# Deadlines for ScalarE's and VectorE's order, and seven products in two of three blocks of one set

## The chip, the core and the metric

The kernel runs on one NeuronCore of one Trainium2 chip. The metric is device time in microseconds (us) of one execution, as the median of several runs; lower is better. Five engines work side by side, each through its own instructions in order: TensorE (PE; its weight loads are listed as PEld), VectorE (DVE), ScalarE (ACT), GpSimd (POOL) and SyncE (SP, which issues most DMAs). They wait for each other by semaphores.

## The reference

Causal attention with a learned decay, then two feed-forward layers, all in fp32:

```python
scores = q @ k.T / sqrt(D) + (cum_i - cum_j)        # cum: running sum of log f, causal mask
x = softmax(scores) @ v                             # 4 x 8 heads, 576 x 64, to 2304 x 512
h = x @ w_in0;  x = (h - tanh(h)) @ w_out0          # 512 -> 2048 -> 512
h = x @ w_in1;  out = (h * sigmoid(h)) @ w_out1     # 512 -> 2048 -> 512
```

## The kernel before

Every large product is made of three products of fp32r parts: each operand is split into a rounded high part (a copy or cast on ScalarE) and the rest (a subtraction on VectorE), and TensorE multiplies high by high, high by low and low by high.

Attention fills about the first 260 us. The two layers follow, in 24 units: unit u is a layer (12 units each), a set of 512 of the 2048 hidden columns (four sets in a layer) and one of three blocks of 768 tokens. Units 0 to 11 are the first layer, 12 to 23 the second; units 12, 13 and 14 are the second layer's first set. Units 0 to 2 run interleaved with the attention's end; `joint()` makes the rest.

A unit's first product (512 model columns to hidden columns, `h_step`, L646) runs as seven block products in place of eight, by Strassen's scheme in Winograd's form: seven steps of 12 matmuls 384 columns wide, on sums of blocks. Its second product (`c_step`, L708) is made in seven steps too where the unit is not in `PLAIN`: 12 matmuls of 384 columns a step in the first layer, 18 of 256 in the second (L729). A unit in `PLAIN` makes it in eight steps without block sums (`plain_c`, L750, matmuls at L769): four steps of 12 matmuls and four of 6, all 512 columns wide, in the second layer. Before, `PLAIN` is units 12 to 14.

In TensorE's order the seven steps of unit u's first product alternate with the seven (or eight) steps of unit u-1's second product, one each in turn. The stretch between the first h_step of unit u and that of unit u+1 is called unit u's stretch below; it holds the second product of unit u-1.

Around this, ScalarE and VectorE do, for each unit:

- bending: the running sums that Winograd's form wants (`seed` and `cp`, copies within PSUM on ScalarE; L1016, L937), Tanh or Silu, and the sums `two` (L940) of bent quarters: two in a plain unit, six in one of seven products;
- splitting the second product's operands into high and low, `gr` (L980 ScalarE, L981 VectorE): four of 768 columns in a plain unit, seven in one of seven products, through a ring of three tiles;
- gathering the second product into `x` (L1016 to L1065), in the first layer's last set with four more sums `mix` (L1047), two of which read a PSUM bank that the next unit's second product will write;
- in units 12 to 14 alone, `make` (L882): two sums (L890) and seven operands `xr` (L905 ScalarE, L902 VectorE), which are spilled to DRAM. Later units load them with a DMA.

Beside this the weights are decoded, once for each chunk q (two chunks to a set) and each matrix m: float64 bits come in by DMA, `scale` (L203) on ScalarE, `shift`, `exponent`, `low`, `join` (L207 to L226) on VectorE, four sums of 256 columns (L230), and the split into high (L247) and low (L249). A plain set's second matrix keeps the undone blocks, without the sums (L239, L241). All decodes share the scratch tiles `wa`, `wb` and `ws`, so they follow one another in the order written.

All of these are written as tasks: the time at which each is wanted (`when`, in steps of 2.08 us), engine, cost, what it reads and writes. `planned` (L1116) puts them in order before the launch. It goes through a model of the engines: TensorE, SyncE and the DMA tasks run in the order of `when`; on VectorE and ScalarE the task that is ready with the least due time is next, where due is `when` plus a hand-set `spare`. Tasks marked `keen` (those that read or write TensorE's banks) may hold an engine idle until they are ready. The order found is what the program issues; at run time each engine keeps it.

```python
now = [n for r, n in known if r <= t]
n = min(now, key=lambda n: tasks[n][7])            # least due
if not tasks[n][6] and tasks[n][7] > t - 2:        # not keen: leave room for a keen one
```

Of the kernel before, what the change touches and what calls it, by code (L numbers as in the profile page):

```python
# [8 lines left out]
F32R = mybir.dt.float32r  # L9
# [29 lines left out]
S0 = U0 // 3  # L39
PLAIN = (12, 13, 14)  # L40
PLAINSETS = {u // NB for u in PLAIN if u >= NB * NSET}
EARLIER = 5
MIXED = {u // NB for u in PLAIN if u < NB * NSET}

# [4 lines left out]
def forgetting_attention_two_ffn(  # L49
# [106 lines left out]
    def wload(q, m, parts=(0, 1)):  # L156
# [20 lines left out]
    )  # L177
# [418 lines left out]
    def ftile(u, what):  # L596
        k = u % 2
        if what == "12":
            if "12" not in small_tiles:
                small_tiles["12"] = pools["xb"].tile([P, 2, 2, TH], F32, tag="xo7", name="f_12")  # L600
            return small_tiles["12"][:, k]
        if what == "21":
            return flat(f"21_{k}", "hp", f"h{k}")
        if what == "1":
            return flat("1", "tp", "t0")
        if what == "22":
            return flat("22", "tp", "t1")
        if what == "tmp":
            if what not in small_tiles:
                g = gfree.pop(0)  # L610
                small_tiles[what] = pools[f"gp{g // 2}"].tile([P, 2, TH], F32, tag=f"gh{g}", name="f_tmp")
                small_tiles["spare"] = g
            return small_tiles[what]
        return flat(what, "xt", {"a": "xt1", "b": "xt2"}[what])
# [49 lines left out]
    def aside_tile():  # L664

        if "tile" not in aside:
            g = small_tiles["spare"]
            aside["tile"] = pools[f"gp{g // 2}"].tile([P, 2, TH], F32, tag=f"gl{g}", name="aside")
        return aside["tile"]
# [40 lines left out]
    def c_step(u, k):  # L710
        l, i = units[u][0], csteps(u)[k]
        t = gtile(gop(u, k))
        if u in PLAIN:
            return plain_c(u, *i, t)
        acc, fresh = cbank(u, i)
        at = WAT[l][i]
        ws = [[w[:, 0] for w in place(2 * (u // NB) + j, at)] for j in range(2)]
        for d in range(3 if l else 2):
            ds = slice(d * P, d * P + P)
            for j, (wh, wl) in enumerate(ws):  # L720
                gh, gl = (t[:, e, j] for e in range(2))
# [12 lines left out]
    def place(q, at):  # L734

        if at >= 11:
            if q % NSLOT < 2:
                return [w[:, 7:8] for w in wtile(q, 0)]
            if "spare" not in wtiles:
                g = small_tiles["spare"]  # L740
                t = pools[f"gp{g // 2}"].tile([P, 2, 256], F32R, tag=f"gl{g}", name="wspare")
                wtiles["spare"] = [t[:, 0:1], t[:, 1:2]]
            return wtiles["spare"]
        return [w[:, at - 8:] for w in extra(q, 1)] if at >= 8 else [w[:, at:] for w in wtile(q, 1)]
# [5 lines left out]
    def plain_c(u, c, a, t):  # L750
# [4 lines left out]
        for d in range(2 - a if l else 2):  # L755
            for j in range(2):
                q = 2 * (u // NB) + j
                gh, gl = (t[:, e, j] for e in range(2))
                if l:
                    ds = slice((2 * a + d) * P, (2 * a + d) * P + P)  # L760
# [35 lines left out]
    def joint():  # L796
# [5 lines left out]

        def task(when, eng, cost, fn, reads=(), writes=(), keen=False, spare=0):

            tasks.append((when, eng, cost, fn, reads, writes, keen, when + spare))

# [16 lines left out]
        def decode(q, m):  # L823
# [17 lines left out]
            groups = [0, 1, 2] if m and q // 2 in MIXED else [0, 1]  # L841
            behind = m and q % 2 and 3 * (q // 2) - 1 in PLAIN
            for g in [1, 3, 4, 5] if behind else groups:
# [4 lines left out]
        def spread(t0, t1, jobs, since):  # L848
# [3 lines left out]
            for e, c, fn, r, w, tag in jobs:  # L852
                if e == "D":
                    task(t - 6, e, c, fn, r, w)
                    continue
                t = max(t, since.get((w[0][:3], tag), t))
                task(t, e, c, fn, r, w, False, 3)
                if e == "V":
                    t += (t1 - t0) * c / total
# [22 lines left out]
        def make(u):  # L882
# [6 lines left out]
            def total(when, to, p, r, op=MINUS):  # L889
                task(t0 + when, "V", W2, lambda: tt_(q[to](), q[p](), q[r](), op), (key[p], key[r]), (key[to],), False, 2)  # L890

# [4 lines left out]
            for k, i in enumerate(STEPS):  # L896
# [7 lines left out]

                task(when, "A", N2, lambda n=n, f=f: copy(ring_tile(n)[:, 0], q[f]()), (key[f],), (kr,), False, 2)  # L905
                task(when + 0.1, "V", W2, low, (key[f], kr), (kr,), False, 2)


        for u in range(U0, len(units) + 1):
            t0 = base[u]  # L910
            if u < len(units):
# [27 lines left out]
                def two(when, to, p, r, op, kt, kp, kr, keen=True):  # L939
                    task(when, "V", W2, lambda: tt_(to, p, r, op), (kp, kr), (kt,), keen, 0 if keen else 2.5)  # L940

# [34 lines left out]
                for k, i in enumerate(order):  # L976
                    n = opno(u) + k
                    g, (frm, kf), kg = gtile(n), src[i], n % 3
                    w = t0 + when[k] + (more if k else 0)
                    task(w, "A", N2, lambda g=g, f=frm: copy(g[:, 0], f), (kf,), (("gh", kg),), False, 2)  # L980
                    task(w + 0.1, "V", W2, lambda g=g, f=frm: tt_(g[:, 1], f, rd(g[:, 0]), MINUS),  # L981
                         (kf, ("gh", kg)), (("gl", kg),), False, 2)
            v = u - 1
# [19 lines left out]
            for k, i in enumerate(csteps(v)):  # L1003
                if plain_:
                    n, kd = gop(v, k), (ky, kz)[i[1]]
                    r = [kd, ("gh", n % 3), ("gl", n % 3)] + [w for j in range(2) for g in (range(1) if l else range(3)) for w in wkeys(q + j, 1, g)]
                    task(t0 + min(2 * k + 1, 14), "P", 1, lambda v=v, k=k: c_step(v, k), r, (kd,))
                    continue
# [3 lines left out]
                when = t0 + k if last else t0 + 2 * k + 1  # L1012
                task(when, "P", 1, lambda v=v, k=k: c_step(v, k), r, (kd,))

# [15 lines left out]
            if l == 0:  # L1030
# [14 lines left out]
                else:  # L1045
                    def mix(when, spare, to, frm, r, op, keys, kt):
                        task(when, "V", W2, lambda: tt_(to() if callable(to) else to, frm, r, op), keys, (kt,), False, spare)  # L1047

                    mix(t0 + 11.5, 4, aside_tile, xs[22], xs[21], MINUS, (kx[22], kx[21]), "aside")
                    mix(t0 + 12.5, 3, xs[22], xs[22], xs[12], PLUS, (kx[22], kx[12]), kx[22])  # L1050
                    mix(t0 + 14.05, 1.2, xs[12], xs[12], ys, MINUS, (kx[12], ky), kx[12])
                    mix(t0 + 14.06, 1.2, xs[21], xs[21], ys, PLUS, (kx[21], ky), kx[21])
                task(t0 + (14.5 if s < NSET - 1 else 13), "S", 0, lambda b=b: aside_store(b), ("aside",), (("t1", b),))
# [62 lines left out]
    def planned(tasks):  # L1116
# [12 lines left out]
        writer, readers, deps = {}, {}, []  # L1129
        for n, (when, eng, cost, fn, reads, writes, keen, due) in enumerate(tasks):  # L1130
            d = {writer[k] for k in reads if k in writer}
# [11 lines left out]
        queue = {e: [n for n, t in enumerate(tasks) if t[1] == e] for e in free}  # L1143

        def ready(n):
            if all(d in end for d in deps[n]):
                return max([end[d] + lag(n, d) for d in deps[n]] + [tasks[n][0] - EARLY])

        while any(queue.values()):
            best = None  # L1150
            for e, waiting in queue.items():
# [4 lines left out]
                now = [n for r, n in known if r <= t]  # L1156
                n = min(now, key=lambda n: tasks[n][7])
                if not tasks[n][6] and tasks[n][7] > t - 2:
                    soon = [r for r, k in known if tasks[k][6] and t < r < t + tasks[n][2] - 0.2]
                    if soon:  # L1160
                        t = min(soon)
                        n = min((k for r, k in known if r <= t and tasks[k][6]), key=lambda n: tasks[n][7])
                if best is None or t < best[0]:
                    best = t, e, n
            t, e, n = best
            queue[e].remove(n)
            end[n] = t + tasks[n][2]
# [441 lines left out]
```

## Time and profile before

| | |
|---|---|
| median of 3 runs | 914.43 us (914.15 to 914.65) |
| the profiled execution | 914.77 us, of which 913.0 us lie between its first and last instruction (the span) |
| TensorE busy, by matmuls | 897.7 us, 98% of the span |
| VectorE busy | 771.3 us, 84% |
| ScalarE busy | 594.6 us, 65% |
| mean granted TensorE clock | 0.996 of full speed |

A matmul's listed duration includes a modelled end that overlaps the next one's start, so the price of a step of several matmuls is read from start to start. VectorE's and ScalarE's listed durations overlap their successors a little too.

### The profile page before, as it was taken

The numbers are of one execution on the slowest core, as the hardware profiler recorded it, in microseconds if no ns is written. First come the engines' busy times: TensorE is split into PE (matmuls) and PEld (weight loads), VectorE is DVE, ScalarE is ACT, GpSimd is POOL, SyncE is SP. The second block draws the span as 40 slices with busy tenths as digits, with TensorE's granted clock in tenths as the row PEclk, the third lists the DMA queues.
The fourth block names the chain that finished last, engine by engine and source line by source line (L and its number), as shares of the span: only waits on it lengthen the run. The fifth ranks groups of instructions, "written<-read, shape, count | busy, mean of one in ns | idle before, by whom it ended". The sixth has DMA issues, their size and how long they took to land.

```text
span 913.0 us, 15853 instructions
## 1 busy us (share of the span) xinstructions
PE 897.7 (98%) x5898; PEld 842.2 (92%) x5898; DVE 771.3 (84%) x1297; ACT 594.6 (65%) x992; POOL 161.3 (18%) x242
## 2 busy tenths in 40 slices
PE   9999999999999999999999989999999999999997
PEld 6777777799999999999999979898899999999997
DVE  7799999789888999998999989875598889876647
ACT  5888888766565767666776767665565566555443
POOL 8999999400000000000000000000000000000000
PEclk9999999999999999999999989999999999999999
DMA  5424533567457777787768656676567666555753
GB/s 164 154 98 155 167 121 103 193 245 314 196 217 265 237 252 259 236 302 280 251 241 287 220 207 252 238 267 235 190 230 282 205 225 225 180 201 176 233 167 117
DMA packets 51101, 196.01 MB, mean 215 GB/s; under 512 B 9744, under 2 KB 15120, under 8 KB 50992
## 3 DMA queue, kind: packets, MB, share of 16 engines
q1 hardware_dynamic: 50744, 194.72, 60.2%
q8 instruction: 46, 0.75, 0.3%
q10 hardware_dynamic: 280, 0.28, 0.1%
q14 instruction: 31, 0.25, 0.1%
HBM read 151.98 MB, written 41.88 MB: 212 GB/s over the span
## 4 chain that ended last, share of the span: by engine, by line
PE 93%; DVE 4%; ACT 2%; issue 1%; POOL 0%; DVEq 0%; ACTq 0%; POOLq 0%
PE h L656 32%; PE a L729 28%; PE a L769 5%; PE s L1294 5%; PE t L1341 5%; PE a L431 5%; PE out_t L1397 5%; PE h L475 3%; PE s L1286 2%; PE h L461 1%; PE out_t L1425 1%; DVE x L1047 1%; DVE gr L981 0%; DVE x L1024 0%; PE out L1397 0%
## 5 line engine op out<-in xcount | busy, mean ns | idle before, releaser
L656 PE MATMUL h<-xr,wh 128*128 128x384 f32 x1176 | 299.8, 335 | 1.0 <-ACT h L937 0.9
L656 PEld LDWEIGHTS h<-xr,wh 128*128 128x128 f32 x1176 | 210.6, 189 | 3.4 <-ACT h L937 1.6
L656 PE MATMUL h<-xr,wl 128*128 128x384 f32 x588 | 197.0, 335 | 0.0
L656 PEld LDWEIGHTS h<-xr,wl 128*128 128x128 f32 x588 | 110.6, 188 | 0.0
L981 DVE TENSOR_TENSOR gr<-f,gr 128x768 fp32r<-128x768 f32 x102 | 97.0, 953 | 14.5 <-ACT gr L980 14.5
L980 ACT CAST gr<-f 128x768 fp32r<-128x768 f32 x102 | 85.5, 838 | 33.3 <-PE a L729 29.5
L1024 DVE TENSOR_TENSOR x<-a,x 128x768 f32<-128x768 f32 (+1 forms) x64 | 59.4, 930 | 28.2 <-PE a L729 27.7
L1315 ACT ACTIVATE p<-p,mn 128x128 f32<-128x128 f32 (+3 forms) x128 | 71.2, 558 | 17.1 <-DVE mn L1307 14.4
L729 PE MATMUL a<-wh,gr 128*128 128x256 f32 x420 | 80.8, 282 | 0.0
L729 PE MATMUL a<-gr,wh 128*128 128x384 f32 x288 | 75.2, 341 | 4.7 <-ACT a L1016 4.1
L1329 POOL TENSOR_SCALAR p<-p,sm 128x128 f32<-128x128 f32 (+3 forms) x128 | 72.7, 584 | 7.7 <-DVE sm L1326 7.2
L1307 DVE CUSTOM_DVE_ANT_0 p<-s,mask 128x128 f32<-128x128 f32 (+3 forms) x128 | 59.6, 479 | 14.3 <-PE s L1294 14.2
L729 PEld LDWEIGHTS a<-wh,gr 128*128 128x128 f32 x420 | 67.5, 190 | 0.0
L1016 ACT COPY a<-a 128x768 f32<-128x768 f32 x43 | 33.7, 784 | 41.8 <-PE a L729 38.5
L729 PE MATMUL a<-weh,gr 128*128 128x256 f32 x312 | 60.2, 282 | 0.3 <-DVE x L1024 0.3
L729 PE MATMUL a<-wl,gr 128*128 128x256 f32 x210 | 59.4, 283 | 0.6 <-DVE wl L249 0.6
L937 ACT COPY h<-h 128x768 f32<-128x768 f32 x42 | 32.9, 784 | 39.6 <-PE h L656 39.2
L729 PEld LDWEIGHTS a<-gr,wh 128*128 128x128 f32 x288 | 53.0, 191 | 5.9 <-ACT a L1016 4.8
L729 PE MATMUL a<-gr,weh 128*128 128x384 f32 x216 | 54.8, 334 | 0.0
L1236 POOL TENSOR_TENSOR kqs<-kqraw,kqs 128x288 fp32r<-128x288 f32 (+1 forms) x62 | 53.8, 889 | 1.3
L937 ACT COPY f<-h 128x768 f32<-128x768 f32 x42 | 33.7, 802 | 30.4 <-PE h L656 22.7
L729 PEld LDWEIGHTS a<-weh,gr 128*128 128x128 f32 x312 | 50.2, 190 | 0.6 <-issue 0.5
(167 smaller groups left out, 2106.3 us busy)
## 6 DMA issues: line engine op xcount, KB each, us to landing
xr<-xd SPq DMA_DIRECT2D x126, 768.0 KB
raw<-w_in SPq DMA_DIRECT2D x32, 512.0 KB
raw<-w_out SPq DMA_DIRECT2D x32, 512.0 KB
xd<-xo SPq DMA_DIRECT2D x21, 768.0 KB
xd<-xr SPq DMA_DIRECT2D x21, 768.0 KB
kqraw<-kq SPq DMA_DIRECT2D x16, 608.0 KB
aside<-aside SPq DMA_DIRECT2D x15, 384.0 KB
vraw<-v SPq DMA_DIRECT2D x16, 320.0 KB
```

The costliest lines, as they stand in the source:

```text
L431: nc.tensor.matmul(dst, w, m, start=first and r == 0, stop=last and r == 2)
L656: nc.tensor.matmul(dst[:, j, 0:TH], w[:, ds], m[:, d], start=i in (1, 5) and d == r == 0, stop=d == 1 and r == 2, skip_group_check=True,)
L729: nc.tensor.matmul(dst, w, m, start=fresh and (l == 0 or d != 1) and j == r == 0, stop=j == 1 and r == 2, skip_group_check=True,)
L769: nc.tensor.matmul(dst, w, m, start=fresh and j == r == 0, stop=last and j == 1 and r == 2, skip_group_check=True)
L937: task(when, "A", N2, lambda: copy(to, frm), (kf,), (kt,), True)
L980: task(w, "A", N2, lambda g=g, f=frm: copy(g[:, 0], f), (kf,), (("gh", kg),), False, 2)
L981: task(w + 0.1, "V", W2, lambda g=g, f=frm: tt_(g[:, 1], f, rd(g[:, 0]), MINUS), (kf, ("gh", kg)), (("gl", kg),), False, 2)
L1024: task(when, "V", n, lambda: tt_(to, *((frm, to) if op == PLUS else (to, frm)), op), (kf, kx[c]), (kx[c],), True)
L1236: eng.tensor_tensor(lo[:, c0:c1], raw[p][:, c0:c1], rd(hi[:, c0:c1]), ALU.subtract)
L1307: nc.vector.tensor_tensor_reduce(out=pt.rearrange("p (g c) -> p g c", g=2) if i == 4 else pt, in0=src, in1=m, op0=ALU.add, op1=ALU.min, sc ...
L1315: nc.scalar.activation(pt, pt, AF.Exp, bias=mn, scale=-1.0, accum_out=sums[:, n // 3 % 5, n % 3, 0:1],)
L1329: nc.gpsimd.tensor_scalar(pt, pt, sm[:, j:j + 1], 1.0, ALU.mult, ALU.mult)
```

## The change

`PLAIN` becomes unit 13 alone. Units 12 and 14 make their second product in seven steps, as later units of the second layer do. Unit 13 still makes all eight block products, but since the set's second matrix is now stored as block sums, with the one undone block that the sums lack kept in a spare column block of the first matrix's tile (`place`), its matmuls are 256 columns wide: 24 in a long step, 12 in a short one. Unit 12's first c_step gains two matmuls of 256 columns that write one whole PSUM bank, and with that waits for what still reads that bank; the previous unit's two last `mix` sums do.

In `planned` the hand-set `spare` is gone. Each ScalarE, VectorE and DMA task gets a latest end: TensorE's tasks have their `when`, and from each task back to what it depends on the cost and the lag are subtracted. The ready task with the least latest end is next; an engine holds for a task that becomes ready soon where that task would miss its latest end behind the chosen one, and the chosen one can wait. This goes for all tasks, of all units from 3 to 23.

```diff
-PLAIN = (12, 13, 14)
-PLAINSETS = {u // NB for u in PLAIN if u >= NB * NSET}
+PLAIN = (13,)
+PLAINSETS = {s for s in range(NSET, 2 * NSET) if all(NB * s + b in PLAIN for b in range(NB))}
-MIXED = {u // NB for u in PLAIN if u < NB * NSET}
+MIXED = {u // NB for u in PLAIN} - PLAINSETS
...
-        (((0, 4, 1),), ((8, 3, 5),), (), ((1, 1, 2),), ((2, 2, 3),), ((0, 1, 1),)),
+        (((0, 4, 1),), ((8, 3, 5),), ((11, 1, 0),), ((1, 1, 2),), ((2, 2, 3),), ((0, 1, 1),)),
...
         acc, fresh = cbank(u, i)
+        if k == 0 and l and units[u - 1][0] == 0:
+
+            w = place(2 * (u // NB), WAT[l][i])[0][:, 0]
+            for c in range(2):
+                nc.tensor.matmul(csums(u)[1][:, 0, 256 * c:256 * c + 256], t[:, 0, 0, 0:P], w, start=c == 0, stop=True,
+                                 skip_group_check=True)
...
         if at >= 11:
-            if q % NSLOT < 2:
-                return [w[:, 7:8] for w in wtile(q, 0)]
...
+            return [w[:, 7:8] for w in wtile(min(q % NSLOT, 1), 0)]
...
+                if l and u // NB in MIXED:
+                    ds = slice((2 * a + d) * P, (2 * a + d) * P + P)
+                    for k, at in enumerate(((11, 1), (0, 2))[i]):
+                        wh, wl = (w[:, 0] for w in place(q, at))
+                        for r, (w, m) in enumerate(((gh[:, ds], wh), (gh[:, ds], wl), (gl[:, ds], wh))):
+                            nc.tensor.matmul(
+                                acc[:, d, 256 * k:256 * k + 256], w, m, start=fresh and j == k == r == 0,
+                                stop=last and j == 1 and r == 2, skip_group_check=True,
+                            )
+                    continue
...
-            tasks.append((when, eng, cost, fn, reads, writes, keen, when + spare))
+            tasks.append((when, eng, cost, fn, reads, writes, keen))
...
-            behind = m and q % 2 and 3 * (q // 2) - 1 in PLAIN
+            behind = m and l and q % 2 and 3 * (q // 2) - 1 in PLAIN and q // 2 not in MIXED
...
-                task(when, "P", 1, lambda v=v, k=k: c_step(v, k), r, (kd,))
+                kd = (kd, kz) if k == 0 and v == NB * NSET and v - 1 not in PLAIN else (kd,)
+                task(when, "P", 1, lambda v=v, k=k: c_step(v, k), r, kd)
...
+        latest = [t[0] if t[1] == "P" else 1e9 for t in tasks]
+        for n in reversed(range(len(tasks))):
+            for d in deps[n]:
+                if tasks[d][1] != "P":
+                    latest[d] = min(latest[d], latest[n] - lag(n, d) - tasks[d][2])
...
-                n = min(now, key=lambda n: tasks[n][7])
-                if not tasks[n][6] and tasks[n][7] > t - 2:
-                    soon = [r for r, k in known if tasks[k][6] and t < r < t + tasks[n][2] - 0.2]
-                    if soon:
-                        t = min(soon)
-                        n = min((k for r, k in known if r <= t and tasks[k][6]), key=lambda n: tasks[n][7])
+                n = min(now, key=lambda n: latest[n])
+
+                soon = [(r, k) for r, k in known if t < r < t + tasks[n][2] - 0.1 and latest[k] + behind < t + tasks[n][2]
+                        and latest[n] + behind > r + tasks[k][2]]
+                if soon:
+                    t, n = min(soon)
```

## Rows read from the trace of the kernel before

**Rows 1.** The page: the span, and each engine's busy us, share and instructions.

```profile
span 913.0 us, 15853 instructions
PE 897.7 (98%) x5898; PEld 842.2 (92%) x5898; DVE 771.3 (84%) x1297; ACT 594.6 (65%) x992; POOL 161.3 (18%) x242
```

**Rows 2.** Windows of units 10 to 13, 15 to 17: start:end, length, busy by engine.

```profile
core 0: us, PE busy (x) PEld busy (x) DVE busy (x) ACT busy (x) POOL busy (x), PEclk, DMA share, GB/s
...
464.62:493.74 29.12, 29.12 (x169) 29.12 (x169) 26.59 (x32) 19.65 (x26) 0.00 (x0) 1.00 0.79 279
493.74:523.60 29.86, 29.40 (x170) 29.08 (x170) 28.19 (x35) 20.33 (x27) 0.00 (x0) 1.00 0.67 234
523.60:560.27 36.67, 32.44 (x169) 31.71 (x169) 33.03 (x39) 24.93 (x31) 0.00 (x0) 0.91 0.51 201
560.27:591.50 31.23, 31.23 (x158) 28.16 (x158) 27.59 (x37) 20.67 (x27) 0.00 (x0) 1.00 0.71 274
...
622.74:653.99 31.25, 31.25 (x158) 28.18 (x156) 15.61 (x20) 15.48 (x19) 0.00 (x0) 1.00 0.61 212
653.99:684.53 30.54, 29.95 (x211) 29.65 (x210) 27.73 (x40) 21.14 (x29) 0.00 (x0) 1.00 0.57 196
684.53:714.17 29.64, 29.64 (x213) 29.64 (x211) 25.11 (x30) 16.45 (x22) 0.00 (x0) 1.00 0.73 261
```

**Rows 3.** Windows, their sum: units 4 to 11, then units 12 to 14.

```profile
sum 233.88, PE 233.42 PEld 232.90 DVE 221.98 ACT 161.15 POOL 0.00; mean PE 29.18 PEld 29.11 DVE 27.75 ACT 20.14 POOL 0.00
...
sum 99.14, PE 94.91 PEld 88.06 DVE 83.65 ACT 66.33 POOL 0.00; mean PE 31.64 PEld 29.36 DVE 27.88 ACT 22.11 POOL 0.00
```

**Rows 4.** Timeline of PE at unit 12's stall: start, us, what, [idle before <-releaser].

```profile
533.66 0.69 PE L729 MATMUL a<-gr,wh 128*128 128x384 f32 x1 [3.66 <-ACT a L1016]
534.92 0.69 PE L729 MATMUL a<-gr,wh 128*128 128x384 f32 x1 [0.58 <-DVE gr L981]
```

**Rows 5.** Windows behind that stall; the granted clock stands third from the end.

```profile
536.00:538.00 2.00, 2.00 (x8) 2.00 (x8) 1.47 (x2) 0.00 (x0) 0.00 (x0) 0.50 0.29 120
```

**Rows 6.** Timeline of ACT there: the copy that TensorE waits for.

```profile
532.80 0.80 ACT L1016 COPY a<-a 128x768 f32<-128x768 f32 x1
```

**Rows 7.** Timeline of DVE there.

```profile
514.19 1.22 DVE L214 SCALAR_TENSOR_TENSOR wb<-raw,wb 128x1024 f32<-128x1024 uint32 x1
...
527.77 0.95 DVE L1047 TENSOR_TENSOR x<-x,a 128x768 f32<-128x768 f32 x1
528.64 0.95 DVE L1047 TENSOR_TENSOR x<-x 128x768 f32<-128x768 f32 x1
529.51 0.95 DVE L902 TENSOR_TENSOR xr<-f_tmp,xr 128x768 fp32r<-128x768 f32 x1
...
530.38 0.95 DVE L1047 TENSOR_TENSOR x<-x,a 128x768 f32<-128x768 f32 x1
...
533.91 0.95 DVE L981 TENSOR_TENSOR gr<-f,gr 128x768 fp32r<-128x768 f32 x1
```

**Rows 8.** Timeline of PE at unit 12's plain steps, then at seven-product steps of unit 16.

```profile
562.36 0.39 PE L769 MATMUL a<-wh,gr 128*128 128x512 f32 x1
...
565.12 0.51 PE L656 MATMUL h<-xr,wh 128*128 128x384 f32 x2
...
567.22 0.39 PE L769 MATMUL a<-wh,gr 128*128 128x512 f32 x1
...
568.61 0.51 PE L656 MATMUL h<-xr,wh 128*128 128x384 f32 x2
...
703.55 0.28 PE L729 MATMUL a<-weh,gr 128*128 128x256 f32 x1
...
705.70 0.52 PE L656 MATMUL h<-xr,wh 128*128 128x384 f32 x2
```

**Rows 9.** Timeline of DVE in unit 14's stretch: weight decoding.

```profile
604.63 1.09 DVE L230 TENSOR_TENSOR ws<-ws 128x256 f32<-128x256 f32 x3
605.64 0.69 DVE L207 TENSOR_SCALAR wa<-raw 128x1024 uint32<-128x1024 uint32 x1
...
607.30 1.23 DVE L214 SCALAR_TENSOR_TENSOR wb<-raw,wb 128x1024 f32<-128x1024 uint32 x1
...
621.23 1.23 DVE L226 TENSOR_TENSOR ws<-wa,wb 128x1024 f32<-128x1024 f32 x1
```

More of the change, by code (lines that the diff above doesn't have):

```diff
@@ L611, in ftile @@
                 small_tiles[what] = pools[f"gp{g // 2}"].tile([P, 2, TH], F32, tag=f"gh{g}", name="f_tmp")
-                small_tiles["spare"] = g
+                small_tiles["aside"] = g
             return small_tiles[what]
@@ L666, in aside_tile @@
         if "tile" not in aside:
-            g = small_tiles["spare"]
+            g = small_tiles["aside"]
             aside["tile"] = pools[f"gp{g // 2}"].tile([P, 2, TH], F32, tag=f"gl{g}", name="aside")
@@ L736, in place @@
         if at >= 11:
-            if q % NSLOT < 2:
-                return [w[:, 7:8] for w in wtile(q, 0)]
[L739 to L743, printed above, removed]
+            return [w[:, 7:8] for w in wtile(min(q % NSLOT, 1), 0)]
         return [w[:, at - 8:] for w in extra(q, 1)] if at >= 8 else [w[:, at:] for w in wtile(q, 1)]
@@ L801, in joint, with task @@
         tt_, copy = nc.vector.tensor_tensor, nc.scalar.copy
-        def task(when, eng, cost, fn, reads=(), writes=(), keen=False, spare=0):
-            tasks.append((when, eng, cost, fn, reads, writes, keen, when + spare))
+        def task(when, eng, cost, fn, reads=(), writes=(), keen=False):
+            tasks.append((when, eng, cost, fn, reads, writes, keen))
         def dve(n):
@@ L856, in spread @@
                 t = max(t, since.get((w[0][:3], tag), t))
-                task(t, e, c, fn, r, w, False, 3)
+                task(t, e, c, fn, r, w)
                 if e == "V":
@@ L889, in total @@
             def total(when, to, p, r, op=MINUS):
-                task(t0 + when, "V", W2, lambda: tt_(q[to](), q[p](), q[r](), op), (key[p], key[r]), (key[to],), False, 2)
+                task(t0 + when, "V", W2, lambda: tt_(q[to](), q[p](), q[r](), op), (key[p], key[r]), (key[to],))
             task(t0 - 4, "D", 3, lambda: aside_load(b, q["11"]()), (("t1", b),), (key["11"],))
@@ L903, in low @@
                     spill(n)
-                task(when, "A", N2, lambda n=n, f=f: copy(ring_tile(n)[:, 0], q[f]()), (key[f],), (kr,), False, 2)
-                task(when + 0.1, "V", W2, low, (key[f], kr), (kr,), False, 2)
+                task(when, "A", N2, lambda n=n, f=f: copy(ring_tile(n)[:, 0], q[f]()), (key[f],), (kr,))
+                task(when + 0.1, "V", W2, low, (key[f], kr), (kr,))
         for u in range(U0, len(units) + 1):
@@ L939, in two @@
                 def two(when, to, p, r, op, kt, kp, kr, keen=True):
-                    task(when, "V", W2, lambda: tt_(to, p, r, op), (kp, kr), (kt,), keen, 0 if keen else 2.5)
+                    task(when, "V", W2, lambda: tt_(to, p, r, op), (kp, kr), (kt,), keen)
                 cp(t0 + 1.05, zs, ys, kz, ky)
@@ L979, in joint @@
                     w = t0 + when[k] + (more if k else 0)
-                    task(w, "A", N2, lambda g=g, f=frm: copy(g[:, 0], f), (kf,), (("gh", kg),), False, 2)
+                    task(w, "A", N2, lambda g=g, f=frm: copy(g[:, 0], f), (kf,), (("gh", kg),))
                     task(w + 0.1, "V", W2, lambda g=g, f=frm: tt_(g[:, 1], f, rd(g[:, 0]), MINUS),
-                         (kf, ("gh", kg)), (("gl", kg),), False, 2)
+                         (kf, ("gh", kg)), (("gl", kg),))
             v = u - 1
@@ L1005, in joint @@
                     n, kd = gop(v, k), (ky, kz)[i[1]]
-                    r = [kd, ("gh", n % 3), ("gl", n % 3)] + [w for j in range(2) for g in (range(1) if l else range(3)) for w in wkeys(q + j, 1, g)]
+                    r = [kd, ("gh", n % 3), ("gl", n % 3)] + [w for j in range(2) for g in (range(1) if q // 2 in PLAINSETS else range(3)) for w in wkeys(q + j, 1, g)]
                     task(t0 + min(2 * k + 1, 14), "P", 1, lambda v=v, k=k: c_step(v, k), r, (kd,))
@@ L1045, in joint, with mix @@
                 else:
[L1046 to L1052, printed above, removed]
+                    def mix(when, to, frm, r, op, keys, kt):
+                        task(when, "V", W2, lambda: tt_(to() if callable(to) else to, frm, r, op), keys, (kt,))
+                    mix(t0 + 11.5, aside_tile, xs[22], xs[21], MINUS, (kx[22], kx[21]), "aside")
+                    mix(t0 + 12.5, xs[22], xs[22], xs[12], PLUS, (kx[22], kx[12]), kx[22])
+                    mix(t0 + 14.05, xs[12], xs[12], ys, MINUS, (kx[12], ky), kx[12])
+                    mix(t0 + 14.06, xs[21], xs[21], ys, PLUS, (kx[21], ky), kx[21])
                 task(t0 + (14.5 if s < NSET - 1 else 13), "S", 0, lambda b=b: aside_store(b), ("aside",), (("t1", b),))
@@ L1129, in planned @@
         writer, readers, deps = {}, {}, []
-        for n, (when, eng, cost, fn, reads, writes, keen, due) in enumerate(tasks):
+        for n, (when, eng, cost, fn, reads, writes, keen) in enumerate(tasks):
             d = {writer[k] for k in reads if k in writer}
@@ L1147, in ready @@
                 return max([end[d] + lag(n, d) for d in deps[n]] + [tasks[n][0] - EARLY])
+        behind = 0
         while any(queue.values()):
@@ L1165, in planned @@
             t, e, n = best
+            if e == "P":
+                behind = t - tasks[n][0]
             queue[e].remove(n)
```

## The prediction, made before the changed kernel ran

> **What bounds the kernel now.** I read the page first: matmuls cover 897.7 of 913.0 us [rows 1]. TensorE is the bound, and everything outside its work is worth at most the 15.3 us in which it shows no matmul, plus what a low clock costs. So a gain must come from fewer or shorter matmuls, or from the few places where TensorE stands.
>
> Then the windows, cut at the first h_step of each unit. A stretch without a wait lasts 29.12 us where both products are in seven steps of the first layer, 29.64 in the second layer, and 31.23 to 31.25 where the second product is plain [rows 2] (the three plain stretches differ by 0.02). Against these three lengths the odd ones stand out: unit 12's stretch takes 36.67, unit 11's 29.86, unit 16's 30.54 [rows 2]. Unit 12's is 7.55 longer than its work.
>
> The timeline of TensorE in unit 12's stretch shows one stall, 3.66 us, and 0.58 us more one matmul later [rows 4]. That is 4.24 of 7.55 us. The remaining 3.3 us are the clock: behind the stall it is granted at 0.50 of full speed, the 1.2 GHz level [rows 5], and each matmul takes twice as long until it is 2.4 GHz again.
>
> What TensorE waited for is a seed copy of ScalarE, which starts at 532.80 [rows 6], and then for a split on VectorE (533.91) [rows 4, 7]. The seed itself could not come sooner because it overwrites a bank that the sums of `mix` for unit 10 read, and the second of these is at 530.38 on VectorE [rows 7]. VectorE was not slow, it was busy with other things: between its two `x<-x,a` lie a sum and an operand that are due later than they, and at 514.19 it had spent 1.22 us on weights of chunk 9's second matrix [rows 7], first used by the plain step at 562.36 [rows 8]. So this is an order that serves the wrong work first, on an engine with little to spare: VectorE is busy 33.03 of these 36.67 us [rows 2].
>
> **TensorE's own work.** Start to start, a long plain step takes 2.76 us (562.36 to 565.12), a short one 1.39 (567.22 to 568.61), a seven-product step of 18 matmuls 2.15 (703.55 to 705.70) [rows 8]. Four long and four short steps make 16.6 us, seven steps 15.05. The windows say the same: 31.23 against 29.64 [rows 2]. Units 12 and 14 therefore give 1.59 and 1.61 us.
>
> Unit 13 gets longer. Its 72 matmuls of 512 columns become 144 of 256, and at 2.15 / 18 = 0.119 us each they take 17.2 us, 0.6 more than 16.6. The two bank-writing matmuls add 0.24. Sum: -1.59 - 1.61 + 0.6 + 0.24 = -2.36 us, about 0.26%. The eighth product that is saved is 12.5% of the columns, but only 9% of the time, because a column costs more in a 256-wide matmul.
>
> A rule speaks to this price. Per matmul the rows show 0.119 us for 256 columns and 2.76 / 12 = 0.230 for 512 [rows 8]. The Trainium skill ("TensorE: Matmul & The Clock Gate", section Back-to-back issue gap) gives a gap of N / 2.4 + 2.5 ns at the fast clock, that is 109 and 216 ns by it. By its figures this sum would be about -3.2 us instead of -2.36, an estimate from that page. The trace does not agree: both forms take 14 and 10 ns more, and the measured price is used.
>
> **The new order.** With latest ends, the `mix` sums of unit 10 inherit the time of the step that waited at 533.66, while weights that are first used 30 us later wait. What VectorE has to do between 523.6 and that step's proper place (529.8) is few things: the two sums, the one split, two or three operands and their difference, at 0.87 us each by their starts (527.77, 528.64, 529.51) [rows 7], about 5.2 of 6.2 us. It fits. I take the whole 7.55 away here and charge what is late next separately. In unit 11 (29.86 against 29.12) and unit 16 (30.54 against 29.64) [rows 2], I take 0.74 and 0.90; the latter came from a special order of chunk 11's weights behind a plain unit 14, which the change drops. Sum -9.19. From below: none of it, if VectorE has no room (a rival below).
>
> **What VectorE gets more of.** A seven-product unit has four more sums (six `two`, not two), three more `gr` splits and one more subtraction in gathering: 8 operations of 768 columns, 7.0 us at 0.87, for unit 12 and again for unit 14. The second matrix of chunks 8 and 9 needs four sums of 256 columns and 1,024 columns more to split: 1.45 (four thirds of 1.09) + 1.22 = 2.7 us each [rows 9, 7]. ScalarE gets three casts, three seeds and 1,024 columns of weights more, about 6 us at some 0.8 us apiece [rows 6]; it is busy 20.67 of 31.23 us in unit 13's stretch [rows 2], and so I charge nothing. That cover goes only if a ScalarE task stands behind a late VectorE task, which is the case that I charge as VectorE's.
>
> Is there room? In the stretches of units 12 to 14 VectorE is busy 83.65 us today [rows 3]. Added and due there: 7.0 (unit 12) + 2.7 (chunk 9), 93.3. Not due before unit 15: the last decode's start, 605.64 to 607.30 (0.69 + 0.69 + 1.23) and 621.23 (1.23) [rows 9], 3.8. So 89.5 us are due. TensorE's work there, without stalls, is 29.12 + 29.64 + 0.24 + 31.25 + 0.6 = 90.85. Only 1.4 us may be idle. Decodes share scratch tiles, so the second matrix of chunk 10 cannot be put behind the first of chunk 11, due when unit 15 starts, and I count none of that as movable.
>
> How much idle time VectorE can't avoid, the eight stretches before bound: 233.88 - 221.98 = 11.9 us [rows 3], 1.5 a stretch, 4.5 in three. Then 3.1 us come back as stalls. The other end is 0, if later deadlines fill every gap (today's idle there, 15.5 us [rows 3], is mostly for want of permitted work, and there will be more of that). I take 2.0, in several short waits, so that the clock holds: waits under 1 us in units 11 and 16 left the clock at 1.00 [rows 2]. If they come as one of some 3 us, 3.3 us of low clock come on top. Unit 14's own additions fall mostly in unit 15's stretch, busy 15.61 of 31.25 [rows 2], where 7.0 more find room.
>
> One wait is added outright. Unit 12's first c_step now follows the two `mix` sums of unit 11 that read the bank which it writes. They can start when unit 11's last c_step is done, and take 1.74 us; TensorE has one h_step, 2.09 us, to cover them. With hand-over at both ends I charge 0.2 us; a 1.22 us decode in front of them would make it 1.0. Behind that c_step queue all of TensorE's later steps, behind the sums VectorE's operands for unit 13.
>
> **Sum.** -2.36 - 9.19 + 2.0 + 0.2 = -9.35 us. The profiled execution took 914.77, so 905.4 by its own time; it lies 0.34 above the median of the runs, against which I predict **905.1 us**. From all work done with no returned wait and some of the shorter waits elsewhere mended too, 901; with 3.1 us returned and one fall of the clock, 909.5. That is the likeliest case's own range.
>
> **Rivals.** About 0.2% (1.8 us) is what a measurement here can tell from no change.
>
> First, the stall in unit 12 stays. VectorE has no idle time from 523 to 537, and 2.7 us of decoding are added around it; if the backlog was built in unit 10 and 11, where VectorE already works 26.59 of 29.12 and 28.19 of 29.86 us [rows 2], a better order finds nothing to put off. Against it: the 1.22 us at 514.19 and the two operations between the sums. Then -2.36 - 0.74 - 0.90 + 0.2: 910.6, and up to 913.3 with the 2.7.
>
> Second, and on the other side: VectorE becomes the bound in units 12 to 14. If nothing can be put off and chunk 8's 2.7 us and three of unit 14's sums (2.6) land there too, 98.6 us are due, with 4.5 idle 103.1 against 90.85: 12.2 us of stalls, and two of them long enough for a low clock, 6.6 more. That gives 914.43 - 11.35 + 18.8 = 921.9. It decides for slower once stalls and low clock in these three stretches pass 13.2 us (11.35 + 1.8). For it: operands of `make` and seven splits now both go through rings of three tiles there. Against it: TensorE runs unhindered in units 4 to 11 with VectorE at 95% [rows 3].
>
> Third, the change doesn't do what it says: the new order differs, but its model's lags are no better than the hand-set ones, and as much is lost in new places as is won in unit 12. Then only -2.36 and the odd microsecond show, 912.6 to 916.3, no change.
>
> **Chances.** Forecast 0.56, all faster; the stall stays 0.20, counted as faster down to 912.6; no change 0.10; VectorE binds 0.14, slower. Faster 0.76, same 0.10, slower 0.14. The range from 901 to 914 leaves out the slow case and slivers on both sides, about 2 in 10.
>
> **What would show it.** In the changed profile, plain matmuls of 512 columns are gone; unit 13's and 15's stretches (second products of 12 and 14) last 29.6 to 29.9 us where nothing waits, unit 14's 31.8; unit 12's falls to 29 to 31 with the clock at 1.00; chunk 9's decoding stands behind unit 10's sums; VectorE is over 95% busy in units 12 to 14. Wrong would be: a wait over 3 us before any c_step or h_step of units 12 to 15, a granted clock of 0.50 anywhere there, or new waits in units 3 to 11, whose order changes too though none of their work does.

## The result, and the profile after

The changed kernel takes 904.32 us (median of four runs, 904.29 to 904.37) against 914.36 for the kernel before in the same session: a ratio of 0.989, with a 95% interval of 0.9873 to 0.9907. The forecast was 905.1 us. The profiled execution took 904.37 us, with a span of 902.6 us, 10.4 less than the 913.0 of [rows 1].

The page after: the span, each engine's busy time, and the granted TensorE clock in 40 slices.

```profile
span 902.6 us, 16281 instructions
PE 890.4 (99%) x6080; PEld 845.5 (94%) x6080; DVE 784.9 (87%) x1321; ACT 602.4 (67%) x1006; POOL 161.6 (18%) x242
PEclk9999999999999999999999999999999999999999
```

TensorE has 182 more matmuls and 7.3 us less busy time; VectorE is busy 13.6 us longer in a shorter span. The clock stays at 0.9 or more in every slice; its mean is 1.000, where it was 0.996.

The windows after, units 11 to 16, which answer to [rows 2]:

```profile
core 0: us, PE busy (x) PEld busy (x) DVE busy (x) ACT busy (x) POOL busy (x), PEclk, DMA share, GB/s
493.36:522.48 29.12, 29.12 (x169) 29.12 (x169) 29.02 (x37) 20.18 (x26) 0.00 (x0) 1.00 0.66 234
522.48:552.31 29.83, 29.40 (x170) 29.08 (x169) 28.56 (x36) 24.09 (x31) 0.00 (x0) 1.00 0.59 230
552.31:583.64 31.33, 30.14 (x213) 29.82 (x213) 30.98 (x40) 24.00 (x32) 0.00 (x0) 1.00 0.61 239
583.64:615.44 31.80, 31.80 (x231) 31.80 (x230) 30.43 (x41) 23.04 (x31) 0.00 (x0) 1.00 0.75 263
615.44:645.07 29.63, 29.63 (x213) 29.63 (x211) 21.56 (x28) 19.44 (x24) 0.00 (x0) 1.00 0.74 258
645.07:674.70 29.63, 29.63 (x212) 29.63 (x211) 28.59 (x38) 21.28 (x27) 0.00 (x0) 1.00 0.63 224
```

Read against [rows 2], unit 12's stretch lost 6.84 us (36.67 to 29.83), unit 11's 0.74 and unit 16's 0.91. Units 13 to 15 took 93.72 us before (31.23, and by the sum of [rows 3] and the row of unit 15 31.24 and 31.25) and take 92.76 now: 0.96 less. Together 9.45 of 10.4 us; the rest is small pieces ahead of these units and in the last stretch.

Two waits remain in these units. The waits of TensorE after (line waited for: us in total, times, longest):

```profile
PE a L720 <- DVE x L1058: 1.2, 1, 1.2
...
PE a L735 <- DVE gr L991: 0.4, 1, 0.4
```

These are idle times as listed. Read from start to start, as stretches beyond their work, the first costs 1.46 us (31.33 in place of 29.87, which is 29.63 and 0.24 for the two bank-writing matmuls) and the second 0.71 (29.83 in place of 29.12).

The first stands before the two bank-writing matmuls of unit 12. On VectorE's timeline after, the split of a weight chunk, the last part of its decoding, stands ahead of the two `mix` sums that they wait for (start, us, what):

```profile
552.74 1.22 DVE L249 TENSOR_TENSOR wl<-ws,wh 128x1024 fp32r<-128x1024 f32 x1
553.88 1.81 DVE L1058 TENSOR_TENSOR x<-x,a 128x768 f32<-128x768 f32 x2
```

TensorE begins at 555.74, when the second sum is done, after 1.19 us of standing.

The other remaining wait comes from ScalarE. Its timeline after, in unit 12's stretch:

```profile
526.84 0.78 ACT L1027 COPY a<-a 128x768 f32<-128x768 f32 x1 [0.55 <-PE a L735]
...
528.92 0.84 ACT L915 CAST xr<-x 128x768 fp32r<-128x768 f32 x1 [0.55 <-PE h L656]
529.78 1.28 ACT L940 ACT_TABLE_LOAD   x1
531.07 0.81 ACT L940 ACTIVATE f<-h 128x768 f32<-128x768 f32 x1
531.78 0.82 ACT L990 CAST gr<-f_b 128x768 fp32r<-128x768 f32 x1
```

VectorE, which makes the low half from this last cast, stands for it:

```profile
532.64 0.96 DVE L991 TENSOR_TENSOR gr<-f_b,gr 128x768 fp32r<-128x768 f32 x1 [1.24 <-ACT gr L990]
```

The seed copy, at 532.80 in [rows 6], now runs at 526.84. What is late now is the cast of `f_b`, behind a cast for `xr` and the change of tables from Tanh to Silu, 1.28 us that `planned` has no task for. Whether such a task would remove the wait was not tried. In the next run, the order alone, the change of tables comes at 528.91, without that cast ahead of it, and nothing waits.

### The profile page after: what moved, and what is told of

Read it like the earlier page. It is cut to its first block, busy times and chain, and to the rows that moved or that the text cites. A ratio compares the mean times of both kernels' runs of the same rounds, so it can differ in the third digit from the quotient of the medians.

```text
span 902.6 us, 16281 instructions
## 1 busy us (share of the span) xinstructions
PE 890.4 (99%) x6080; PEld 845.5 (94%) x6080; DVE 784.9 (87%) x1321; ACT 602.4 (67%) x1006; POOL 161.6 (18%) x242
## 4 chain that ended last, share of the span: by engine, by line
PE 94%; DVE 3%; ACT 1%; issue 1%; POOL 0%; DMA 0%; DVEq 0%; POOLq 0%; ACTq 0%
PE h L656 33%; PE a L735 32%; PE t L1362 5%; PE s L1315 5%; PE a L431 5%; PE out_t L1418 5%; PE h L475 3%; PE a L764 2%; PE s L1307 2%; PE h L461 1%; PE out L1418 0%; PE out_t L1446 0%; DVE x L1035 0%; ACT raw L203 0%; DVE gr L991 0%
## 5 line engine op out<-in xcount | busy, mean ns | idle before, releaser
L735 PE MATMUL a<-wh,gr 128*128 128x256 f32 x516 | 99.2, 282 | 0.0
L735 PEld LDWEIGHTS a<-wh,gr 128*128 128x128 f32 x516 | 82.9, 190 | 0.0
L735 PE MATMUL a<-weh,gr 128*128 128x256 f32 x384 | 74.0, 282 | 0.3 <-DVE x L1035 0.3
L735 PE MATMUL a<-gr,wh 128*128 128x384 f32 x288 | 73.3, 334 | 0.4 <-DVE gr L991 0.4
L735 PE MATMUL a<-wl,gr 128*128 128x256 f32 x258 | 72.8, 282 | 0.0
L1027 ACT COPY a<-a 128x768 f32<-128x768 f32 x49 | 38.4, 783 | 47.1 <-PE a L735 45.5
L735 PEld LDWEIGHTS a<-weh,gr 128*128 128x128 f32 x384 | 61.7, 190 | 0.6 <-issue 0.5
L735 PE MATMUL a<-wel,gr 128*128 128x256 f32 x192 | 54.2, 282 | 0.0
```

What stands on the lines that cost most here:

```text
L735: nc.tensor.matmul(dst, w, m, start=fresh and (l == 0 or d != 1) and j == r == 0, stop=j == 1 and r == 2, skip_group_check=True,)
```

## The experiments

**The order alone.** The changed kernel with units 12 to 14 plain:

```diff
-PLAIN = (13,)
+PLAIN = (12, 13, 14)
```

> Only the new order; units 12 to 14 stay plain. Theory (the order mends the stall, the products give TensorE's 2.4 us by themselves): unit 12's stretch falls from 36.67 to 29.1 to 30 us with no low clock, unit 11's to 29.12; unit 16's stretch keeps its 0.9 us, which hangs on a plain unit 14. About 906.5 us. Rival (it is the lighter second products that free the engines, the order matters little): the stall stays above 3 us and the time above 911.

904.78 us (904.47 to 905.97), ratio 0.9896 (0.9883 to 0.991). The windows, units 12 to 14 and 16:

```profile
522.44:551.56 29.12, 29.12 (x170) 29.12 (x169) 28.33 (x34) 24.47 (x32) 0.00 (x0) 1.00 0.58 221
551.56:582.78 31.22, 31.22 (x158) 28.16 (x157) 30.63 (x41) 22.04 (x29) 0.00 (x0) 1.00 0.79 294
582.78:614.02 31.24, 31.24 (x157) 28.18 (x156) 22.55 (x29) 20.04 (x26) 0.00 (x0) 1.00 0.70 263
...
645.27:674.92 29.65, 29.65 (x211) 29.64 (x210) 25.45 (x37) 21.68 (x28) 0.00 (x0) 1.00 0.59 201
```

There is no wait left in any of them, nor in unit 15's (31.25). The order by itself is worth the whole of unit 12's 7.55 us. Unit 16's 0.9 us go too, with unit 14 still plain and chunk 11's weights in their special order: this part of the expectation was wrong. And the products add almost nothing on top: the spans of the profiled executions are 902.8 and 902.6 us, and the two intervals overlap.

**The products alone.** All of the change except the task times and `planned`, which stay as before (`spare`, least due time).

> Only the seven products in units 12 and 14; the order is found with the hand-set due times of before. Theory: the stall in unit 12 stays or grows by up to the 2.7 us of added decoding; TensorE's work falls by 2.4 us, unit 16's 0.9 us go; new waits in units 13 and 14, because VectorE has 7 us more to do under the old order: 911 to 917 us. Rival (the products are what won): 906 us or less.

917.13 us (916.07 to 918.24), ratio 1.0031 (1.002 to 1.0042): slower by 0.3%, just above what was expected. The waits of TensorE, and the windows of units 12, 13 and 16:

```profile
PE a L720 <- DVE x L1058: 4.3, 1, 4.3
PE a L735 <- ACT a L1027: 3.4, 2, 2.9
...
PE a L735 <- DVE gr L991: 1.7, 1, 1.7
```

```profile
523.33:559.89 36.56, 31.94 (x169) 31.31 (x169) 34.04 (x44) 25.45 (x33) 0.00 (x0) 0.91 0.49 191
559.89:595.85 35.96, 31.69 (x214) 31.28 (x213) 34.09 (x43) 24.63 (x33) 0.00 (x0) 0.95 0.68 249
...
657.27:686.90 29.63, 29.63 (x212) 29.63 (x211) 27.42 (x38) 20.70 (x27) 0.00 (x0) 1.00 0.62 218
```

The old stall costs as much as before (36.56 us; it is now 2.94 us for the seed and 1.68 for the split), and under the old order the bank-writing matmuls wait 4.27 us for the two `mix` sums, with a second fall of the clock behind them (0.95 over the stretch). The 2.4 us of TensorE's work are saved and 6.1 are lost in unit 13. Unit 16's stretch has no wait here, under the old order: the products, which drop the special order of chunk 11's weights, remove it as the new order does. Either part is enough for these 0.9 us.

**Three due times by hand.** The kernel before, with the two `mix` sums that read the bank, and the low half of unit 11's second split, due earlier:

```diff
-                    mix(t0 + 14.05, 1.2, xs[12], xs[12], ys, MINUS, (kx[12], ky), kx[12])
-                    mix(t0 + 14.06, 1.2, xs[21], xs[21], ys, PLUS, (kx[21], ky), kx[21])
+                    mix(t0 + 14.05, -1.5, xs[12], xs[12], ys, MINUS, (kx[12], ky), kx[12])
+                    mix(t0 + 14.06, -1.5, xs[21], xs[21], ys, PLUS, (kx[21], ky), kx[21])
...
-                         (kf, ("gh", kg)), (("gl", kg),), False, 2)
+                         (kf, ("gh", kg)), (("gl", kg),), False, -0.5 if u == 11 and k == 1 else 2)
```

> The kernel before with three due times moved: the two mix sums that the seed waits for, and the low half of unit 11's second split, are due 2.5 to 2.7 steps sooner. Nothing else changes. Theory (the stall is the order's fault, VectorE has room): the 3.66 us wait and the low clock go, unit 12's stretch 29.1 to 30.5 us, 907 to 908.5 us. Rival (VectorE is full there): the wait moves to the next steps, unit 12's stretch stays over 33 us and the time over 911.

913.37 us (912.45 to 914.57), ratio 0.9988 (0.9979 to 0.9997). The wait is 3.66 us as before, unit 12's stretch 35.5 us. VectorE's timeline there:

```profile
525.71 0.95 DVE L981 TENSOR_TENSOR gr<-f,gr 128x768 fp32r<-128x768 f32 x1
526.58 0.95 DVE L1047 TENSOR_TENSOR aside<-x 128x768 f32<-128x768 f32 x1
...
528.32 0.95 DVE L1047 TENSOR_TENSOR x<-x,a 128x768 f32<-128x768 f32 x1
529.18 0.95 DVE L1047 TENSOR_TENSOR x<-x 128x768 f32<-128x768 f32 x1
...
530.92 0.95 DVE L1047 TENSOR_TENSOR x<-x,a 128x768 f32<-128x768 f32 x1
```

The split moved from 533.91 [rows 7] to 525.71. The two sums came no sooner: `aside<-x` and `x<-x` read what they overwrite, must run first, and still had their late due times. So I had read [rows 7] wrongly in one point: the sum between the two was no later work that got in front, but work that the second depends on.

**Due times of all four sums.** The same, with these two moved as well (`4` to `1` and `3` to `0`).

> The kernel before with the three due times of the run on three due times and those of the two other mix sums moved too. These two must run ahead of the sums that the seed waits for, since they read what those overwrite; in the run on three due times they stayed late and held the others. Theory (a due time by hand does not reach a task's predecessors, the latest ends do): all four run together early, the 3.66 us wait falls under 1 us, no low clock, unit 12's stretch under 30.5 us, 907 to 909 us. Rival (VectorE has no room, whatever the order): the wait moves on, unit 12's stretch over 33 us, 911 us or more.

910.75 us (910.52 to 911.14), ratio 0.9959 (0.9946 to 0.9972). VectorE's timeline, then ScalarE's, then TensorE's waits, then the window of unit 12:

```profile
521.08 0.95 DVE L1047 TENSOR_TENSOR aside<-x 128x768 f32<-128x768 f32 x1
...
522.82 0.95 DVE L1047 TENSOR_TENSOR x<-x 128x768 f32<-128x768 f32 x1
523.69 1.81 DVE L1047 TENSOR_TENSOR x<-x,a 128x768 f32<-128x768 f32 x2
```

```profile
527.15 0.78 ACT L1016 COPY a<-a 128x768 f32<-128x768 f32 x1 [1.25 <-PE a L729]
527.84 0.79 ACT L937 COPY h<-h 128x768 f32<-128x768 f32 x1
```

```profile
528.69 0.61 PE L656 MATMUL h<-xr,wh 128*128 128x384 f32 x2 [1.58 <-ACT h L937]
...
531.71 0.45 PE L729 MATMUL a<-gr,wh 128*128 128x384 f32 x1 [0.47 <-DVE gr L981]
...
536.92 0.44 PE L729 MATMUL a<-gr,wh 128*128 128x384 f32 x1 [0.77 <-DVE gr L981]
```

```profile
522.79:555.59 32.80, 29.98 (x170) 29.02 (x169) 29.77 (x36) 23.51 (x31) 0.00 (x0) 1.00 0.55 206
```

Now all four are done by 525.5 in place of 531.3 [rows 7], the 3.66 us wait and the low clock are gone, and 3.9 of 7.55 us are won. The rest, 3.7 us, is three new waits. The longest, 1.58 us, no due time on VectorE reaches: on ScalarE the seed, which waits for TensorE, stands ahead of the copy that the next h_step needs. The two others are for splits on VectorE that are late next. Neither my size (907 to 909) nor the rival's (911 and more) was met. What holds is that this stall was the order's fault; what fell is that moving one chain is enough. The next chain is late behind it, and of the orders run here only the one in which every task carries the deadline of what follows it cleared them all (29.12 us with the order alone, on the same work).

**The hold left out.** The changed kernel without the four lines from `soon = [...` to `t, n = min(soon)`.

> The changed kernel without the rule by which an engine holds for a task that becomes ready soon: it takes the ready task with the least latest end, always. Theory (the latest ends worked back through the tasks do the work, the hold is a trifle): 903.5 to 906 us. Rival (the hold is what keeps TensorE from waiting): waits in many units, 908 us or more.

904.87 us (904.82 to 904.93), ratio 0.9895 (0.9883 to 0.9908): 0.5 us more than the changed kernel by the medians. The same two waits of TensorE are left in units 12 and 13, 0.7 us each as listed. The latest ends do the work.

**The clock by itself.** The kernel before with matmuls that nobody reads ahead of the step that waits in unit 12 (`c_step`, u = 11, k = 1). First 40 of them into the bank `chain(u)[0]`, with start flags; this kernel's outputs come out otherwise, so only its times are read:

```diff
+        if u == NB * NSET - 1 and k == 1:
+            for n in range(40):
+                nc.tensor.matmul(chain(u)[0][:, 0, TH:512], ws[0][0][:, 0:P], ws[0][0][:, 0:P], start=True, stop=True,
+                                 skip_group_check=True)
```

> The kernel before with 40 matmuls of 128 columns that nobody reads put on TensorE in front of the step that waits 3.66 us in unit 12. They write columns of a PSUM bank that hold nothing. Theory (3.3 of the 7.55 us are the low clock behind the stall, and it falls because TensorE stands): the clock holds at 1.00, unit 12's stretch about 33.4 us, 911.0 us. Rival (the clock falls for another reason, or the loss is the wait alone): unit 12's stretch stays at 36.5 us or grows, 914.4 us or more.

918.79 us (913.93 to 920.27), and nothing decided: the fill itself had to wait, as TensorE's timeline and a window behind its start show.

```profile
531.96 8.48 PE L720 MATMUL h<-wh 128*128 128x128 f32 x40 [2.24 <-ACT f L934]
```

```profile
535.00:538.00 3.00, 3.00 (x16) 3.00 (x16) 2.20 (x3) 0.15 (x1) 0.00 (x0) 0.50 0.29 121
```

Then 30 of them, without start flags, into the other bank:

```diff
+            for n in range(30):
+                nc.tensor.matmul(chain(u)[1][:, 0, TH:512], ws[0][0][:, 0:P], ws[0][0][:, 0:P], start=False, stop=True,
+                                 skip_group_check=True)
```

> As the filled stall, with 30 matmuls into a bank that no pending ScalarE task reads (the 40 of the run before waited 2.24 us for a Silu themselves, and the clock fell all the same). Theory (3.3 of the 7.55 us are the low clock, which falls because TensorE stands): the fill runs from 529.9 on, the clock holds at 1.00, unit 12's stretch 33.4 us, 911.0 us. Rival (the loss is the wait alone, or the clock falls anyhow): 36 us or more, 914 us or more.

912.12 us (911.95 to 913.49), ratio 0.9978 (0.9969 to 0.9987). TensorE's timeline, a window behind its start, and that of unit 12:

```profile
529.97 3.46 PE L720 MATMUL h<-wh 128*128 128x128 f32 x30
533.79 0.44 PE L733 MATMUL a<-gr,wh 128*128 128x384 f32 x1 [0.36 <-ACT a L1020]
535.06 0.44 PE L733 MATMUL a<-gr,wh 128*128 128x384 f32 x1 [0.83 <-DVE gr L985]
```

```profile
536.00:540.00 4.00, 4.00 (x25) 4.00 (x24) 4.00 (x5) 1.43 (x2) 0.00 (x0) 1.00 0.48 197
...
523.73:557.88 34.15, 32.96 (x200) 32.57 (x199) 32.88 (x39) 24.96 (x31) 0.00 (x0) 1.00 0.57 220
```

The useful matmul starts no sooner than in [rows 4] (533.79 against 533.66), but at 536 the clock stands at 1.00 where [rows 5] have 0.50. Unit 12's stretch takes 34.15 us in place of 36.67. So 2.5 us of the 7.55 were the low clock (2.2 by the medians), where I had worked out 3.3, and the other 5.0 were the waits themselves: the 4.24 us of [rows 4] are idle times as listed, and these leave out the modelled ends of the matmuls before them.

**The bank written later.** The changed kernel with the two bank-writing matmuls of `c_step` behind the loop over `d` instead of ahead of it; the step's own 18 matmuls don't touch that bank.

> The changed kernel, with the two matmuls that write the bank moved behind the 18 matmuls of the same step instead of ahead of them. Theory (1.19 us of TensorE's wait there are for the two mix sums alone): the wait goes under 2.15 us of matmuls, unit 13's stretch falls from 31.33 to about 29.9 us, 903.0 us. Rival (the next thing, the split for that step or the seed copy, ends the wait just as late): 904.3 us, the same.

903.57 us (903.52 to 903.87), ratio 0.9882 (0.9867 to 0.9897). The wait for the sums is gone. The waits of TensorE and the window of unit 13:

```profile
PE h L656 <- DVE xr L912: 0.5, 1, 0.5
```

```profile
552.23:582.84 30.61, 30.14 (x214) 29.88 (x213) 30.58 (x39) 23.95 (x32) 0.00 (x0) 1.00 0.60 234
```

Half of the 1.46 us is won (31.33 to 30.61); the other half comes back one step on, where the operand that VectorE makes next is late. VectorE is busy 30.58 of 30.61 us. The two matmuls themselves take the 0.24 us that were charged (556.46 to 556.70 on this run's timeline). This version has the least median of those run. Its lead over the changed kernel stands in the spans of the two profiled executions (901.8 and 902.6 us) and the medians, which were taken in different sessions; the two intervals overlap, so it is likely and not settled.

**No plain unit.** `PLAIN = ()` in the changed kernel.

> The changed kernel with no plain unit: unit 13 too makes its second product in seven steps. TensorE has 2.2 us less work (unit 14's stretch 29.63 in place of 31.80), VectorE 7.0 us more in the stretches of units 13 to 15. Theory (VectorE is nearly full in the stretches of units 12 to 14, 89.97 of 92.96 us busy): waits of 3 us or more come in units 14 and 15, 905 to 911 us. Rival (there is room, since 8 us are idle in unit 15's stretch): 902.1 us.

904.87 us (904.58 to 905.14), ratio 0.9895 (0.9883 to 0.9908). The windows of units 14 and 15:

```profile
582.71:615.19 32.48, 30.14 (x212) 29.74 (x211) 32.10 (x43) 25.21 (x33) 0.00 (x0) 1.00 0.60 212
615.19:645.89 30.70, 29.99 (x212) 29.65 (x211) 25.64 (x34) 21.92 (x30) 0.00 (x0) 1.00 0.83 297
```

TensorE's 2.2 us are saved, and units 14 and 15 lose 2.8 and 1.1 us: 32.48 and 30.70 where the work is 29.63. VectorE is busy 32.10 of 32.48. The waits are those expected, the time just under the lower end of the range, since unit 12's stretch lost its 0.7 us (29.12). The work of that stretch is the same as in the changed kernel, so the 0.7 us hung on how the order fell and not on VectorE's load. With the bank-writing matmuls moved as well:

> No plain unit, and the two bank-writing matmuls behind their step's others: the run with all seven lost 1.07 us before them and 2.9 us of waits in units 14 and 15 against 2.2 us of TensorE's work saved. Theory (VectorE is at its limit, a wait that goes in unit 13 comes back later in part): 903.8 to 904.8 us, no better than the plain unit 13 with the same move (903.57). Rival (the waits are independent): 903.0 us or less.

904.29 us (903.71 to 904.86), ratio 0.9889 (0.9876 to 0.9903): no better than a plain unit 13 with that move.

**Unit 12 plain in place of 13.** `PLAIN = (12,)` in the changed kernel; it leaves out the two bank-writing matmuls, and with them what they prepare for the set's later sums, so only its times are read.

> The changed kernel with unit 12 as the plain one in place of unit 13: the same amount of work, 7 us of VectorE's moved from unit 12's and 13's stretches (where waits of 0.71 and 1.46 us remain) to unit 14's, and no bank-writing matmuls with their wait. Theory (these remaining waits come from VectorE being fullest where unit 11's mix sums, unit 12's sums and unit 13's operands meet): both go, 902.2 to 903 us. Rival (the 7 us make new waits of the same size one unit later): 904 us or more.

904.07 us (903.98 to 904.15), ratio 0.9887 (0.9872 to 0.9902). The windows of units 13 and 14:

```profile
552.58:584.36 31.78, 31.78 (x229) 31.78 (x229) 30.45 (x39) 23.22 (x31) 0.00 (x0) 1.00 0.76 277
584.36:615.09 30.73, 29.91 (x213) 29.59 (x211) 30.26 (x39) 24.82 (x32) 0.00 (x0) 1.00 0.63 235
```

Unit 13's wait goes, unit 12's 0.7 us stay (29.85), and 1.1 us are lost in unit 14 (30.73 where the work is 29.63). The rival's time was met, if only just: most of what unit 13 gives back is lost one unit later.

## Why the prediction came out

**TensorE's work** was -2.36 us. Taking 1.46 us of waiting from unit 13's stretch, units 13 to 15 have 29.87 + 31.80 + 29.63 = 91.3 us of work against 93.72: -2.4. The price per matmul that was read from start to start held. (Of the two excesses over the cited gap that the prediction names, 10 ns belong to 256 columns and 14 to 512.)

**The order's share** was -9.19, unit 12 taken whole and the new waits charged apart. Units 11 and 16 gave 0.74 and 0.91; unit 12 gave 7.55 with the order alone. So the mechanism held, a wrong order on an engine with room, but several of its reasons need mending. The late sum between the two `mix` sums was a predecessor of the second (three due times). With it and `aside<-x`, the list of what VectorE must do between 523.6 and 529.8 is eight operations, some 7.0 us at 0.87, and would not fit into 6.2; the changed order had run these two before the stretch began, at 519.91 and 521.65. One reordered chain gave half (all four sums): what pays is that every task inherits a deadline, on ScalarE too. There the seed of [rows 6] started 1.5 us after the last sum ended (531.33), behind the change of tables, a Silu and a cast:

```profile
531.38 0.81 ACT L930 ACTIVATE f<-h 128x768 f32<-128x768 f32 x1
532.08 0.82 ACT L905 CAST xr<-x 128x768 fp32r<-128x768 f32 x1
```

And unit 16's wait goes not only when the special order of chunk 11's weights is dropped (products alone, as predicted) but with the new order too. The low clock was a cause of its own, as said, at 2.5 us and not 3.3; the waits' share was so much larger.

**What comes back** was 2.0 us in units 12 to 14 for want of VectorE's time and 0.2 for the new dependency. Measured are 0.71 in unit 12 and 1.46 at the dependency, 2.17 in all: the sum is right and the parts are not, which is luck. The dependency was mis-sized; I had named a decode in front of the sums as its upper bound (1.0), and that is what happened, at 1.46, with `x<-x` just ahead of it up to 552.7; the rule by which an engine holds did not keep the sums' place free. The 0.71 us came from ScalarE, which had been charged nothing: VectorE stood there and waited for its cast. So for want of VectorE's time alone little came back in the changed kernel, and where the bank is written later, half of the 1.46 did. The room itself was sized well: 89.5 us due, 89.97 busy (28.56 + 30.98 + 30.43).

**Elsewhere** 0.9 us more were won than counted (10.4 less 9.45), in pieces of 0.2 us in unit 7's stretch and before unit 3, and 0.6 in the last stretch. That is about the difference between 905.1 and 904.3. The piece before unit 3 lies ahead of all that was put in a new order, and none of the three was traced to a cause.

**The rivals.** The products without the new order ended on the side of the rival that VectorE binds in units 12 to 14, at 917.13 us. But there too the order had its part: on VectorE's timeline the two sums that TensorE waited for, at 561.94 and 565.41, had three other operations between them, of which the second needed one. With the new order VectorE is 97% busy in these stretches (89.97 of 92.96), near that limit, and the two runs that took or moved more of TensorE's work there got it back as waits. That the stall stays for want of room is refuted by the order alone. The two parts of the change don't add up: order alone -9.9 us, products alone +2.5, both -10.0, each against the kernel before in its own session.

## What to carry to other kernels

Before a due time is tuned by hand, follow the waiting step back through everything that it depends on, over all engines: a deadline on the last task alone leaves its predecessors late, and mending one chain uncovers the next. Work taken from the bounding engine is worth only what the second engine can carry in that stretch, in time; here 2.4 us of matmuls, paid for with work on a VectorE that had an estimated 1.4 us to spare, gave 0.2 us by the spans, and 1.0 with the bank-writing matmuls moved out of the way. Where a wait cannot be removed, look at what it does to the clock behind it, which here cost 2.5 us on top of 5.0 us of waiting.

## What was not expected of the hardware

The clock fell behind a wait shorter than that in [rows 4]. In the first filled stall TensorE stood 2.24 us, and the granted clock was 0.50 from 535 to 538 although matmuls ran without a gap from 531.96 on; those were 128 columns wide. Nor does the same program always end alike: one of that kernel's seven executions took 913.93 us at a mean clock of 0.999, the six others 918.68 to 920.27 at 0.992 to 0.994. With all four sums moved TensorE stood 1.58 us and the window kept 1.00. What between these decides whether the clock falls, and whether the narrow matmuls behind the wait had a part in it, these runs don't tell.
